# Turned tiles moved one place, LayerNorm sums of later tokens on ScalarE, last stores by SyncE and ScalarE

## The chip, the cores and the metric

The kernel runs on one core of one Trainium2 chip. The metric is the device time of one execution in microseconds (us). Engines are named as in the profile: PE (TensorE, matrix products), PEld (its weight loads), DVE (VectorE), ACT (ScalarE), POOL (GpSimd), SP (SyncE, which here only issues DMA transfers).

## The reference

Two rounds of attention and feed-forward over 2048 tokens of width 576. Each of the four steps adds to x what it computes from the normalised x. Attention has 32 heads of 18 columns; a token sees itself and seven earlier ones at distances 2, 4, ..., 14. The feed-forward part (FFN) has 4608 inner columns. All is fp32, with one core and batch 1.

```python
D, S, H, Dh, W, dil, F = 576, 2048, 32, 18, 8, 2, 4608

def _A_ref(x, wqkv, wo):
    qkv = (x @ wqkv).reshape(B, S, 3, H, Dh).transpose(2, 0, 3, 1, 4)
    q, k, v = qkv
    idx = arange(S)[:, None] - (arange(W) * dil)[None, :]          # masked where negative
    logits = einsum("bhsd,bhswd->bhsw", q, k[:, :, idx]) * Dh ** -0.5
    o = einsum("bhsw,bhswd->bhsd", softmax(logits), v[:, :, idx])
    return o.transpose(0, 2, 1, 3).reshape(B, S, D) @ wo

def _B_ref(x, w1, w2):
    return silu(x @ w1) @ w2

x = x + _A_ref(layernorm(x), wqkv, wo)
x = x + _B_ref(layernorm(x), w1, w2)
x = x + _A_ref(layernorm(x), wqkv, wo)      # the same weights again
x = x + _B_ref(layernorm(x), w1, w2)
```

## The kernel before

**Stages.** The tokens are cut into four chunks of 512, and a chunk into four tiles of 128 tokens. A stage s (0 to 7) is one chunk in one layer: s = 0 to 3 are the chunks of layer 0, 4 to 7 those of layer 1. A stage does LayerNorm, qkv (line 707), attention on DVE, the projection with its own transposes ("project", line 876), a second LayerNorm ("LN(s)" below), and the FFN. Every fp32 operand of a matmul is split into two f16 halves, and a product takes three f16 passes: high with high, high with low, low with high. A tile's normalised tokens yh (high and low half) are turned, that is transposed, before they can enter a product: by PE and a copy on ACT (lines 441 and 443) or by a DMA of SP (line 445).

**Chunk 0's stage carries more.** While attention of chunk 0 runs on DVE, PE computes qkv for chunks 1, 2 and 3 ahead (`qkv_ahead`, line 707 with `ra`, `rb`, `h` or `wo` as weights). So the LayerNorms of all four chunks (x, x1, x2, x3 in `front(0)`) come early, and DVE has the statistics of all of them. Then comes project(0), LN(0) and the first FFN.

**FFN.** Stages 0 to 2 use the plain form: line 1137 multiplies a tile of 128 inner columns (56 matmuls are four such tiles), ACT applies SiLU (line 1139), ACT and DVE split the result into halves (lines 1044 and 1046), and line 1150 accumulates the second product into `acc`, which DVE adds to x (line 883). From stage 3 on a cheaper form (`pair_z`, line 1064) uses prepared weights that `prepare` makes during the earlier stages. In the first FFN the weights are raw: POOL loads them (line 910), ACT squares and sums them for a scale (lines 931 and 933), PE adds over partitions (line 936), DVE rounds to powers of two (lines 413 to 415), then ACT and DVE write the two halves (lines 944 to 951).

**LayerNorm's forms.** `layer_norm(xs, prio, into, on_act, ...)`: with `on_act` False, DVE does the statistics (lines 469 and 470) and the normalisation (548, 553 and 428). With True, statistics are on DVE, and ACT shifts and scales (562 and 565), with the low half on DVE (428). With 2, ACT sums too: a Copy pass with an accumulator for the sum, the mean of all four tiles on DVE, and then a Square pass for the variance (the function `total`). `into` names the place that the turned tokens take.

**Places.** One large tile of SBUF (`rb`) is cut in several ways (`shared`); the cuts overlap, and a buffer may take a place only when whatever overlaps it has been read. XW is the size of one chunk's turned tokens. Chunks 0 to 3 of the qkv stage take the three places of "xa" in turn, (0, XW), (XW, 2XW), (2XW, 3XW), so that chunk 3 gets (XW, 2XW). The FFN's turned tokens take "x0", "x1", "x2". In LN the first write of a chunk (the key "hold" on the first operation of the normalisation) already claims the place.

**Order.** No order is written by hand. Every operation is given to a planner (`Plan`) with an engine, a cost in us, what it reads and writes, a priority and buffers. The planner simulates the engines, picks for each engine the ready operation of best priority, and gives the buffers out in turns. The order in which it picks is the order of each engine's queue. On the chip an engine runs its queue in that order and waits only for data and places.

Of the kernel before, what the change touches and what calls it, by code (L numbers as in the profile page):

```python
# [278 lines left out]
def sliding_attention_silu_ffn(ctx: ExitStack, tc: tile.TileContext, x, wqkv, wo, w1, w2, out):  # L279
# [637 lines left out]
    def raw_split(f0, prio):  # L917
# [11 lines left out]
        for f in fs:  # L929
            a, b = raws[f]  # L930
            op("ACT", 0.95, lambda f=f: nc.scalar.activation(junk[:, 0:640], fl(ra(f)), AF.Square,
                                                             accum_out=accw[:, f, 0:1]), [a], [("accw", f, 0)], prio)
            op("ACT", 0.9, lambda f=f: nc.scalar.activation(junk[:, 0:D], rb(f), AF.Square,
# [8 lines left out]
        for f, (wa, wb) in zip(fs, wab):  # L942
            a, b = raws[f]
            op("ACT", 0.82, lambda f=f, wa=wa: nc.scalar.activation(T(wa)[:, 0:5, :], ra(f), AF.Copy,
                                                                    scale=s12[:, f, 0:1]), [a, ("s12", f)], [(wa, 0)], prio)
            op("DVE", 0.9, lambda f=f, wa=wa: nc.vector.scalar_tensor_tensor(
                T(wa)[:, 5:10, :], ra(f), s12[:, f, 0:1], T(wa)[:, 0:5, :], op0=ALU.mult, op1=ALU.subtract),
               [a, (wa, 0), ("s12", f)], [(wa, 1)], prio)
            op("ACT", 0.77, lambda f=f, wb=wb: nc.scalar.activation(T(wb)[:, 0, :], rb(f), AF.Copy,
                                                                    scale=s12[:, f, 1:2]), [b, ("s12", f)], [(wb, 0)], prio)  # L950
            op("DVE", 0.83, lambda f=f, wb=wb: nc.vector.scalar_tensor_tensor(
# [147 lines left out]

    def ffn(s, xT, xs):  # L1100
# [4 lines left out]
        for g in range(NFT // n):  # L1105
# [8 lines left out]
            for f in range(g * n, (g + 1) * n):  # L1114
# [24 lines left out]
                op("ACT", 0.7, lambda z=z, hs=hs, f=f: nc.scalar.activation(T(hs), T(z), AF.Silu, scale=r12[:, f, 0:1]),  # L1139
                   [z, ("s12", f)], [(hs, 0), (hs, 1)], pd, table="silu")  # L1140
# [18 lines left out]
        for j in range(NJ):  # L1159
# [3 lines left out]
            else:  # L1163
                op("POOL", 0.6, lambda j=j: nc.gpsimd.dma_start(x_rows(out, c, j), T(xs[j])), [xs[j]], [], pd,  # L1164
                   nbytes=P * D * 4)
# [93 lines left out]
```

## Time and profile before

| | before |
|---|---|
| median of 3 runs | 2170.06 us (2168.5 to 2170.9) |
| profiled execution, device time | 2170.76 us |
| its span in the profile | 2169.0 us |
| mean granted clock of PE | 0.995 |
| PE busy | 2116.9 us (98%), 15676 matmuls |
| DVE busy | 1623.5 us (75%) |
| ACT busy | 958.4 us (44%) |
| POOL busy | 455.3 us (21%) |

The span runs from the first to the last instruction that the profile shows. Busy times are sums over one engine. A row of the waits names the engine that waited, line and operand, after `<-` who released it, and then the total, how often, and the longest. In a timeline the first number is the start, the second the duration of the whole group `xN` of equal instructions, and the bracket at the end the idle time before it with its releaser. A row of instruction groups ends with busy time and mean ns of one, and with the idle time of the engine before them. Rows that name a `DRAIN` or a semaphore belong to an engine's sequencer and not to its busy time.

### The profile page before, as it was taken

Reading aid. Unit: us, or ns where it says so; the run is one execution under the profiler, and the core shown is the slowest. Engines: PE = TensorE matmul, PEld = TensorE weight load, DVE = VectorE, ACT = ScalarE, POOL = GpSimd, SP = SyncE. Lnnn points to the kernel's source line nnn. Section 1 sums busy time; section 2 is a strip of 40 time slices with the busy share of each in tenths; the row PEclk is TensorE's granted clock in tenths of the full one; section 3 lists DMA queues with packets and bytes.
Section 4 is the critical chain, followed back from the end, with each engine's and each line's share of the span. In section 5 each row is a group of like instructions: output and inputs, shape, how many; then the busy total and the mean of one; then the engine's idle time right before and its main releaser. Section 6 shows DMA issues by size and latency. Waiting matters only on the chain.

```text
span 2169.0 us, 39537 instructions
## 1 busy us (share of the span) xinstructions
PE 2116.9 (98%) x15676; PEld 1529.5 (71%) x15676; DVE 1623.5 (75%) x2541; ACT 958.4 (44%) x1685; POOL 455.3 (21%) x713
## 2 busy tenths in 40 slices
PE   5999899999999999999999999999999999999998
PEld 3555556656666665677787778877788778888886
DVE  7999799999999986679974798629974398733332
ACT  7544877553244434364432544324434345324431
POOL 3234455310355654631000110000000100000000
PEclk9999899999999999999999999999999999999999
DMA  7778567776688879796458855676557665555541
GB/s 198 198 204 270 194 223 249 239 226 198 198 239 261 254 180 236 232 298 201 130 160 221 250 171 166 151 256 180 155 150 222 195 188 153 156 161 178 181 150 41
DMA packets 296217, 429.08 MB, mean 198 GB/s; under 512 B 150480, under 2 KB 182076, under 8 KB 291552
## 3 DMA queue, kind: packets, MB, share of 16 engines
q1 hardware_dynamic: 251360, 301.53, 48.2%
q0 software_dynamic: 42656, 123.93, 18.2%
q8 instruction: 122, 2.00, 0.4%
q10 hardware_dynamic: 2016, 1.11, 0.2%
q14 instruction: 63, 0.52, 0.1%
HBM read 303.19 MB, written 72.40 MB: 173 GB/s over the span
## 4 chain that ended last, share of the span: by engine, by line
PE 65%; issue 18%; DVE 8%; DMA 5%; ACT 1%; POOL 1%; SPq 0%; ACTq 0%; POOLq 0%; DVEq 0%
PE acc L1150 28%; PE z L1064 14%; PE z L1137 13%; PE z L707 7%; PE acc L876 3%; DMA rb<-in_B_w_dram 1%; DVE lg L808 1%; DVE pr L837 1%; DMA w<-in_B_w_dram 1%; DVE pr L844 1%; DMA w<-wts 1%; DVE pr L804 1%; DVE yh L428 1%; DMA w<-in_A_wqkv_dram 0%; DVE st L469 0%
## 5 line engine op out<-in xcount | busy, mean ns | idle before, releaser
L1150 PE MATMUL acc<-w,h 128*128 128x288 f16 x6912 | 881.5, 286 | 0.2 <-DVE x L883 0.2
L1150 PEld LDWEIGHTS <-h 128*128 128x128 f16 x6912 | 676.1, 98 | 172.5 <-issue 0.4
L1064 PE MATMUL z<-rb,w 128*128 128x256 f16 (+1 forms) x4410 | 518.9, 272 | 2.4 <-ACT hs L1069 1.4
L1064 PEld LDWEIGHTS <-w 128*128 128x128 f16 (+1 forms) x4410 | 429.0, 97 | 68.7 <-issue 1.9
L1137 PE MATMUL z<-rb,w 128*128 128x512 f16 x1512 | 334.5, 381 | 2.7 <-ACT rb L443 1.4
L883 DVE SCALAR_TENSOR_TENSOR x<-acc,d,x 128x576 f32<-128x576 f32 x192 | 156.2, 814 | 174.4 <-PE acc L1150 173.7
L1044 ACT ACTIVATE h<-hs,sh 128x512 f16<-128x512 f32 x288 | 201.2, 718 | 181.0 <-PE acc L1150 175.4
L707 PEld LDWEIGHTS <-rb 128*128 128x128 f16 x1792 | 175.6, 98 | 149.2 <-issue 6.6
L1137 PEld LDWEIGHTS <-w 128*128 128x128 f16 x1512 | 148.4, 98 | 176.5 <-issue 6.4
L1046 DVE SCALAR_TENSOR_TENSOR h<-hs,sh,h 128x512 f16<-128x512 f32 x288 | 208.6, 747 | 63.0 <-ACT h L1044 61.8
L1072 DVE TENSOR_TENSOR hs<-z,hs 128x256 f32<-128x256 f32 x270 | 110.2, 419 | 175.8 <-PE z L1064 105.6
L707 PE MATMUL z<-ra,rb 128*128 128x432 f16 x1176 | 224.8, 347 | 2.3 <-ACT qt L775 2.2
L1069 ACT ACTIVATE hs<-z 128x256 f32<-128x256 f32 x270 | 97.6, 379 | 228.8 <-PE z L1064 218.7
L837 DVE TENSOR_TENSOR pr<-kv,pe 128x1152 f32<-128x1152 f32 x128 | 170.2, 1351 | 0.7
L804 DVE TENSOR_TENSOR pr<-qt,kv 128x2304 f32<-128x2304 f32 x64 | 163.2, 2551 | 5.1 <-DMA kv<-kv 3.5
L808 DVE TENSOR_REDUCE lg<-pr 128x128 f32<-128x2304 f32 x64 | 162.9, 2545 | 0.5
L1076 ACT ACTIVATE hs<-hs,dt 128x256 f32<-128x256 f32 (+1 forms) x180 | 109.5, 612 | 89.7 <-DVE hs L1072 89.4
L1139 ACT ACTIVATE hs<-z,r 128x512 f32<-128x512 f32 x108 | 73.9, 685 | 167.1 <-PE z L1137 166.4
L1164 POOL DMA_DIRECT2D out_dram<-x x16 | 8.8, 552 | 652.0 <-DVE x L883 652.0
L844 DVE TENSOR_TENSOR pr<-pr 128x1152 f32<-128x1152 f32 (+1 forms) x128 | 135.1, 1055 | 3.2
L876 PE MATMUL acc<-wo,oT 128*128 128x288 f16 x896 | 113.5, 286 | 0.0
L773 ACT ACTIVATE kv<-z,ru 128x288 f32<-128x288 f32 x80 | 39.6, 495 | 156.1 <-PE z L707 156.1
(212 smaller groups left out, 1785.6 us busy)
## 6 DMA issues: line engine op xcount, KB each, us to landing
w<-wts SPq DMA_DIRECT2D x270, 320.0 KB
w<-w2s SPq DMA_DIRECT2D x252, 288.0 KB
w<-w1s SPq DMA_DIRECT2D x72, 320.0 KB
kv<-kd SPq DMA_DIRECT2D x12, 1584.0 KB
ra<-wqs SPq DMA_DIRECT2D x17, 1080.0 KB
w<-wts SPq DMA_DIRECT2D x90, 160.0 KB
w1s<-w POOLq DMA_DIRECT2D x36, 320.0 KB, 3.6
w2s<-w POOLq DMA_DIRECT2D x36, 288.0 KB, 4.1
```

Of the source, the lines that this page charges most:

```text
L707: nc.tensor.matmul(T(m)[:, :3 * UC], a, b, start=n == 0, stop=n == len(pl) - 1)
L804: nc.vector.tensor_tensor(T(pr), T(qt)[:, j:j + 2, None, :].to_broadcast([P, 2, W, UC]), win(T(kv), j, 2), op=ALU.mult)
L808: nc.vector.tensor_reduce(T(lg)[:, j:j + 2].rearrange("p a w h -> p (a w h)"), T(pr).rearrange("p a w (h d) -> p (a w h) d", d=DH), axis=A ...
L837: nc.vector.tensor_tensor(T(pr)[:, a].rearrange("p w (h d) -> p w h d", d=DH), v, T(pe)[:, j + a, :, :, None].to_broadcast([P, W, UH, DH]) ...
L844: nc.vector.tensor_tensor(t[:, :, 0:h, :], t[:, :, 0:h, :], t[:, :, h:2 * h, :], op=ALU.add)
L876: nc.tensor.matmul(T(acc)[:, h, 0:288], a, b[:, h * 288:(h + 1) * 288], start=n == 0, stop=n == len(pl) - 1)
L883: nc.vector.scalar_tensor_tensor(t, T(acc)[:, :, 0:288], d, t, op0=ALU.mult, op1=ALU.add)
L1044: op("ACT", 0.72, lambda: nc.scalar.activation(T(h)[:, 0, :], T(hs), AF.Copy, scale=sh[:, f:f + 1]), [(hs, 0), (hs, 1), key], [(h, 0)], pd)
L1046: op("DVE", 0.75, lambda: nc.vector.scalar_tensor_tensor(T(h)[:, 1, :], T(hs), sh[:, f:f + 1], T(h)[:, 0, :], op0=ALU.mult, op1=ALU.subtract),
L1064: nc.tensor.matmul(T(z)[:, 0:HT], T(w[m // 2])[0:q, 2 * j + m % 2 if m < 6 else j, :], T(xT)[0:q, 5 * c + i, :], start=first and n == 0, s ...
L1137: nc.tensor.matmul(T(z), v, u, start=m == 0, stop=m == len(pl) - 1)
L1150: nc.tensor.matmul(T(acc)[:, h, 0:288], T(hb[q])[:, a, j * P:(j + 1) * P], T(wbs[q][0])[:, w, h * 288:(h + 1) * 288], start=q == 0 and m = ...
```

## The change

There are four parts.

1. The places. Chunk 3's turned tokens get a tag of their own, "xb", with the place that they had before. Chunk 0's turned tokens for the FFN move from (XW, 2XW) to (0, XW), which was chunk 0's place in the qkv stage, and x1 and x2 change accordingly, with the third place of the prepared weights "pw".
2. LayerNorm. The sums of chunk 2 (ahead), chunk 3 and LN(0) go from DVE to ACT (`on_act` 2); LN(0)'s normalisation goes to ACT too, but for the low half.
3. The planner's costs are written anew for some twenty operations (a few lines are shown). They change no operation, but the whole order.
4. The end. The last tile's accumulation is done by column halves, each with its own add and its own store, one by SP and one by ACT; the other three stores of the last chunk go from POOL to SP.

```diff
-        ("x0", [(XW, 2 * XW)], cut(9), True),
-        ("x1", [(0, XW)], cut(9), True),
-        ("x2", [(35 * HT, 35 * HT + XW)], cut(9), True),
+        ("xb", [(XW, 2 * XW)], cut(9), True),
+        ("x0", [(0, XW)], cut(9), True),
+        ("x1", [(XW, 2 * XW)], cut(9), True),
+        ("x2", [(2 * XW, 3 * XW)], cut(9), True),
...
-        ("pw", [("ra", 0, 30 * P), (3 * XW, 3 * XW + 30 * P), (XW, XW + 30 * P)], lambda v: v, True)])
+        ("pw", [("ra", 0, 30 * P), (3 * XW, 3 * XW + 30 * P), (0, 30 * P)], lambda v: v, True)])
...
-                op("DVE", 1.15, lambda j=j: stats(j), [xs[j]], [(st, j), (mv, j)], prio)
+                op("DVE", 0.95, lambda j=j: stats(j), [xs[j]], [(st, j), (mv, j)], prio)
...
-            op("DVE", 1.25 if blk == 0 else 0.9, soft_a, [], lgs + [mx], pr_)
+            op("DVE", 1.43 if blk == 0 else 1.02, soft_a, [], lgs + [mx], pr_)
...
+    def last(acc, j, g, n, hb, wbs, pp, pd, xs):
+        for h in range(2):
+            sl = slice(h * 288, (h + 1) * 288)
+            def mm(h=h, sl=sl):
+                for q in range(n):
+                    for m, (a, w) in enumerate(((0, 0), (0, 1), (1, 0))):
+                        nc.tensor.matmul(T(acc)[:, h, 0:288], T(hb[q])[:, a, j * P:(j + 1) * P], T(wbs[q][0])[:, w, sl],
+                                         start=q == 0 and m == 0, stop=q == n - 1 and m == 2)
+            op("PE", 0.37 * n, mm, ..., [(acc, h)], pp)
+            op("DVE", 0.46, lambda h=h, sl=sl: nc.vector.scalar_tensor_tensor(
+                T(xs[j])[:, sl], T(acc)[:, h, 0:288], d2[:, g:g + 1], T(xs[j])[:, sl], op0=ALU.mult, op1=ALU.add),
+               [(acc, h), ("sh", g), xs[j]], [(xs[j], h)], pd)
...
+            op(("SP", "ACT")[h], 0.5, lambda h=h, sl=sl, o=o: (nc.sync, nc.scalar)[h].dma_start(o, T(xs[j])[:, sl]),
+               [(xs[j], h)], [], pd, nbytes=P * D * 2)
...
+                if s == NL * NC - 1 and g == NFT // n - 1 and j == NJ - 1:
+                    last(acc, j, g, n, hb, wbs, pp + LATE, pd, xs)
+                    continue
...
-            else:
+            elif s < NL * NC - 1:
                 op("POOL", 0.6, lambda j=j: nc.gpsimd.dma_start(x_rows(out, c, j), T(xs[j])), [xs[j]], [], pd,
                    nbytes=P * D * 4)
+            elif j < NJ - 1:
+                op("SP", 0.5, lambda j=j: nc.sync.dma_start(x_rows(out, c, j), T(xs[j])), [xs[j]], [], pd,
+                   nbytes=P * D * 4)
...
-            x2 = layer_norm(load_x(2, -2.0, gate[3:4]), -2.0, "xa", True, PE_LN[2])
+            x2 = layer_norm(load_x(2, -2.0, gate[3:4]), -2.0, "xa", 2, PE_LN[2])
...
-            x3 = layer_norm(load_x(3, -1.2, gate[11:12]), -1.2, "xa", True, PE_LN[3])
+            x3 = layer_norm(load_x(3, -1.2, gate[11:12]), -1.2, "xb", 2, PE_LN[3])
...
-        XT[s] = layer_norm(X[s], s - 1.0, "xt" if s >= SF else f"x{s}", (False, True, False, False)[min(s, 3)], s == 0)
+        XT[s] = layer_norm(X[s], s - 1.0, "xt" if s >= SF else f"x{s}", (2, True, False, False)[min(s, 3)], s == 0)
```

**How the order moves at LN(0).** ACT's queue before, from the last copies of chunk 3's qkv (`hs<-z`, line 720) on; `rb<-acc` copies a turned tile, `junk,accw<-` squares raw weights:

```order
L720 ACTIVATE hs_119<-z_129,ru 128x432
L720 ACTIVATE hs_122<-z_130,ru 128x432
L443 ACTIVATE rb<-acc_134 128x9x128
L931 ACTIVATE junk,accw<-rb 128x640
L443 ACTIVATE rb<-acc_133 128x9x128
L933 ACTIVATE junk,accw<-rb 128x576
```

The four copies of turned tiles stand behind all qkv copies. The same place in the changed kernel, ACT (lines are one or two numbers higher; `y<-x,nt` and `yh<-y,nt` are the normalisation):

```order
L721 ACTIVATE hs_119<-z_130,ru 128x432
L444 ACTIVATE rb<-acc_134 128x9x128
L563 ACTIVATE y_87<-x_69,nt_127 128x576
L566 ACTIVATE yh_89<-y_87,nt_127 128x576
L721 ACTIVATE hs_121<-z_129,ru 128x432
L444 ACTIVATE rb<-acc_133 128x9x128
L721 ACTIVATE hs_120<-z_130,ru 128x432
L444 ACTIVATE rb<-acc_134 128x9x128
L828 ACTIVATE pe_84<-lg_82 128x256
L1160 ACT_TABLE_LOAD
L1160 ACTIVATE hs_119<-z_129,r_296 128x512
```

Copies of qkv tiles and of turned tiles now alternate, and the first SiLU (line 1160) follows the last of them behind one exponential of attention(1). DVE before, from the end of LN(0)'s Newton steps (`nt`) to the first tile's low half (line 428):

```order
L496 SCALAR_TENSOR_TENSOR nt_127<-nt_127 128x4
L837 TENSOR_TENSOR pr_79<-kv_76,pe_83 128x1152 x2
L844 TENSOR_TENSOR pr_79<-pr_79 128x2x576
L844 TENSOR_TENSOR pr_79<-pr_79 128x2x288
L845 TENSOR_TENSOR o_78<-pr_79 128x2x144
L837 TENSOR_TENSOR pr_79<-kv_76,pe_83 128x1152 x2
L548 TENSOR_SCALAR y_87<-x_66,mv_125,nt_127 128x576
L553 TENSOR_SCALAR yh_88<-y_87 128x576
L428 SCALAR_TENSOR_TENSOR yh_88<-y_87,yh_88 128x512
```

DVE in the changed kernel, the same place:

```order
L497 SCALAR_TENSOR_TENSOR nt_127<-nt_127 128x4
L845 TENSOR_TENSOR pr_79<-pr_79 128x2x576
L845 TENSOR_TENSOR pr_79<-pr_79 128x2x288
L846 TENSOR_TENSOR o_78<-pr_79 128x2x144
L429 SCALAR_TENSOR_TENSOR yh_88<-y_87,nt_127,yh_88 128x512
L429 SCALAR_TENSOR_TENSOR yh_88<-y_87,nt_127,yh_88 128x64
L805 TENSOR_TENSOR pr_79<-qt_81,kv_77 128x2304
L429 SCALAR_TENSOR_TENSOR yh_89<-y_87,nt_127,yh_89 128x512
```

Less attention work stands between Newton's last step and the first tile, and the two high-half operations are gone from DVE.

**Behind the first FFN tiles.** ACT in the changed kernel, from the third SiLU on; `w_94` and `w_100` are the weights of the fifth and sixth FFN tile:

```order
L1160 ACTIVATE hs_121<-z_129,r_296 128x512
L934 ACTIVATE junk,accw<-rb 128x576
L932 ACTIVATE junk,accw<-ra 128x640
L1160 ACTIVATE hs_120<-z_130,r_296 128x512
L934 ACTIVATE junk,accw<-rb 128x576
L945 ACTIVATE w_94<-rb,s_295 128x640
L950 ACTIVATE w_104<-rb,s_295 128x576
L945 ACTIVATE w_100<-rb,s_295 128x640
```

The weights of the fifth tile are written behind the fourth SiLU and the last square; before, they were written ahead of the first SiLU. PE's two sums for these scales (line 937) stand behind the fourth tile's matmuls.

**The end.** SP's last rows in the changed kernel (before, its queue ended with the two weight loads, and POOL's with four stores of 128x576):

```order
L894 DMA w_106<-w2s_227 128x1152
L894 DMA w_109<-w2s_228 128x1152
L1191 DMA out_dram<-x_70 128x576
L1191 DMA out_dram<-x_71 128x576
L1191 DMA out_dram<-x_72 128x576
L1118 DMA out_dram<-x_73 128x288
```

The other half of x_73 is ACT's last row.

More of the change, by code (lines that the diff above doesn't have):

```diff
@@ L809, in red @@
                                             T(pr).rearrange("p a w (h d) -> p (a w h) d", d=DH), axis=AX.X, op=ALU.add)
-                op("DVE", 2.57, mul, keys + [(qt, j), (qt, j + 1)], [pr], pr_)
-                op("DVE", 2.57, red, [pr], [(lg, j)], pr_)
+                op("DVE", 2.5, mul, keys + [(qt, j), (qt, j + 1)], [pr], pr_)
+                op("DVE", 2.5, red, [pr], [(lg, j)], pr_)
             def soft_a(lg=lg, mx=mx):
@@ L930, in raw_split @@
             a, b = raws[f]
-            op("ACT", 0.95, lambda f=f: nc.scalar.activation(junk[:, 0:640], fl(ra(f)), AF.Square,
+            op("ACT", 0.88, lambda f=f: nc.scalar.activation(junk[:, 0:640], fl(ra(f)), AF.Square,
                                                              accum_out=accw[:, f, 0:1]), [a], [("accw", f, 0)], prio)
-            op("ACT", 0.9, lambda f=f: nc.scalar.activation(junk[:, 0:D], rb(f), AF.Square,
+            op("ACT", 0.82, lambda f=f: nc.scalar.activation(junk[:, 0:D], rb(f), AF.Square,
                                                             accum_out=accw[:, f, 1:2]), [b], [("accw", f, 1)], prio)
@@ L943, in raw_split @@
             a, b = raws[f]
[L944 removed]
+            op("ACT", 0.74, lambda f=f, wa=wa: nc.scalar.activation(T(wa)[:, 0:5, :], ra(f), AF.Copy,
                                                                     scale=s12[:, f, 0:1]), [a, ("s12", f)], [(wa, 0)], prio)
[L946 removed]
+            op("DVE", 0.81, lambda f=f, wa=wa: nc.vector.scalar_tensor_tensor(
                 T(wa)[:, 5:10, :], ra(f), s12[:, f, 0:1], T(wa)[:, 0:5, :], op0=ALU.mult, op1=ALU.subtract),
                [a, (wa, 0), ("s12", f)], [(wa, 1)], prio)
[L949 removed]
+            op("ACT", 0.69, lambda f=f, wb=wb: nc.scalar.activation(T(wb)[:, 0, :], rb(f), AF.Copy,
                                                                     scale=s12[:, f, 1:2]), [b, ("s12", f)], [(wb, 0)], prio)
[L951 removed]
+            op("DVE", 0.74, lambda f=f, wb=wb: nc.vector.scalar_tensor_tensor(
                 T(wb)[:, 1, :], rb(f), s12[:, f, 1:2], T(wb)[:, 0, :], op0=ALU.mult, op1=ALU.subtract),
@@ L1043, in halves @@
     def halves(f, hs, h, key, pd):
-        op("ACT", 0.72, lambda: nc.scalar.activation(T(h)[:, 0, :], T(hs), AF.Copy, scale=sh[:, f:f + 1]),
+        op("ACT", 0.66, lambda: nc.scalar.activation(T(h)[:, 0, :], T(hs), AF.Copy, scale=sh[:, f:f + 1]),
            [(hs, 0), (hs, 1), key], [(h, 0)], pd)
-        op("DVE", 0.75, lambda: nc.vector.scalar_tensor_tensor(
+        op("DVE", 0.69, lambda: nc.vector.scalar_tensor_tensor(
             T(h)[:, 1, :], T(hs), sh[:, f:f + 1], T(h)[:, 0, :], op0=ALU.mult, op1=ALU.subtract),
@@ L1071, in add @@
         def add(z, t, s, k):
-            op("DVE", 0.43, lambda: nc.vector.tensor_tensor(T(t)[:, s], T(z)[:, 0:HT], T(t)[:, s], op=ALU.add),
+            op("DVE", 0.36, lambda: nc.vector.tensor_tensor(T(t)[:, s], T(z)[:, 0:HT], T(t)[:, s], op=ALU.add),
                [z], [(t, k)], pd - 0.2)
@@ L1098, in pair_z @@
             halves(f, t, h, key, pd)
+    def last(acc, j, g, n, hb, wbs, pp, pd, xs):
[6 more added lines that the diff above has]
+                                         start=q == 0 and m == 0, stop=q == n - 1 and m == 2)
+            op("PE", 0.37 * n, mm, [(hb[q], a) for q in range(n) for a in range(2)] + [k for q in range(n) for k in wbs[q][1]],
+               [(acc, h)], pp)
+            op("DVE", 0.46, lambda h=h, sl=sl: nc.vector.scalar_tensor_tensor(
+                T(xs[j])[:, sl], T(acc)[:, h, 0:288], d2[:, g:g + 1], T(xs[j])[:, sl], op0=ALU.mult, op1=ALU.add),
+               [(acc, h), ("sh", g), xs[j]], [(xs[j], h)], pd)
+            o = x_rows(out, NC - 1, j)
+            o = bass.AP(tensor=o.tensor, offset=o.offset + h * 288, ap=[o.ap[0], [1, 288]])
+            op(("SP", "ACT")[h], 0.5, lambda h=h, sl=sl, o=o: (nc.sync, nc.scalar)[h].dma_start(o, T(xs[j])[:, sl]),
+               [(xs[j], h)], [], pd, nbytes=P * D * 2)
     def ffn(s, xT, xs):
```

4 lines of the change are left out of this document (2 added, 2 removed).

## The prediction

> **What bounds the kernel now.** I read the busy time of each engine by stretches first, because it shows in one table where TensorE does not work. Columns: stretch and its length; busy time and instructions of PE, weight loads, DVE, ACT and POOL; granted clock; DMA share; GB/s.
>
> ```profile
> 0.00:200.00 200.00, 175.65 (x1026) 99.23 (x1027) 180.58 (x316) 112.64 (x220) 61.53 (x100) 1.00 0.76 216
> 150.00:200.00 50.00, 48.89 (x332) 30.71 (x331) 48.94 (x67) 25.90 (x45) 18.52 (x33) 1.00 0.75 254
> 200.00:250.00 50.00, 37.27 (x188) 18.54 (x187) 40.22 (x69) 27.50 (x47) 20.17 (x34) 0.83 0.56 182
> 250.00:2150.00 1900.00, 1895.22 (x14396) 1405.01 (x14395) 1400.33 (x2156) 818.25 (x1419) 371.98 (x578) 1.00 0.67 198
> 2150.00:2169.00 19.00, 8.73 (x72) 6.75 (x69) 2.40 (x3) 0.00 (x0) 1.62 (x3) 0.87 0.11 47
> ```
>
> For 1900 us in the middle PE is the bound: it misses 4.8 us in all. No matmul is removed, so only the 52 us in which PE idles can be won: 24.4 before 200, 12.7 from 200 to 250, 10.3 at the end. The waits of PE and its timeline say what the 12.7 are (columns of the waits: total, times, longest).
>
> ```profile
> PE acc L441 <- DVE yh L553: 8.1, 4, 3.1
> PE z L1137 <- ACT rb L443: 1.4, 1, 1.4
> ```
> ```profile
> 202.35 10.38 PE L707 MATMUL z<-ra,rb 128*128 128x432 f16 x56
> 214.55 0.40 PE L441 MATMUL acc<-ident,yh 128*128 128x128 f16 x4 [1.82 <-DVE yh L553]
> 215.41 0.45 PE L441 MATMUL acc<-ident,yh 128*128 128x128 f16 x5 [0.47 <-DVE yh L428]
> 227.79 0.61 PE L441 MATMUL acc<-ident,yh 128*128 128x128 f16 x4 [0.34 <-DVE yh L553]
> 230.87 14.44 PE L1137 MATMUL z<-rb,w 128*128 128x512 f16 x56 [1.43 <-ACT rb L443]
> 245.15 0.28 PE L936 MATMUL z<-accw,ones 128*128 128x4 f32 x2
> 245.29 6.20 PE L1137 MATMUL z<-rb,w 128*128 128x512 f16 x28
> ```
>
> After the last of chunk 3's qkv tiles (212.7) PE has only chunk 0's LN transposes, and DVE hands them over one at a time until the first FFN matmul at 230.87. That matmul stretch is slow too: its 56 matmuls take 14.44, where the next 28 take 6.20, so 12.4 for 56. The 2.0 are the low clock (0.83 in this stretch). Why DVE is late stands in its own timeline:
>
> ```profile
> 205.47 0.16 DVE L496 SCALAR_TENSOR_TENSOR nt<-nt 128x4 f32<-128x4 f32 x1
> 205.55 2.62 DVE L837 TENSOR_TENSOR pr<-kv,pe 128x1152 f32<-128x1152 f32 x2
> 213.43 0.57 DVE L548 TENSOR_SCALAR y<-x,mv,nt 128x576 f32<-128x576 f32 x1
> 227.84 0.83 DVE L428 SCALAR_TENSOR_TENSOR yh<-y,yh 128x512 f16<-128x512 f32 x2
> ```
>
> The statistics are complete at 205.6, yet the normalisation starts at 213.43, behind attention work and 0.7 after the last matmul that reads chunk 3's turned tokens, whose place chunk 0's were to take. That is the "hold" in the code.
>
> **The change part by part.** *The new places and ACT for LN(0).* The order now has LN(0)'s transposes between the last four qkv tiles, and the first FFN matmul right behind the fourth transposition. Up to PE's 1536th row both orders read nearly alike, and there project(0) begins earlier by four qkv tiles:
>
> ```profile
> 164.51 10.38 PE L707 MATMUL z<-rb 128*128 128x432 f16 x56
> 174.73 1.17 PE L441 MATMUL acc<-ident,yh 128*128 128x128 f16 x18
> 173.33 1.80 DVE L428 SCALAR_TENSOR_TENSOR yh<-o,so,yh 128x512 f16<-128x512 f32 x4
> ```
>
> So PE asks for project(0)'s first tile at 164.5 and not at 174.7. Can DVE deliver? Durations (busy total, mean ns; the row of POOL is a load with its time to landing):
>
> ```profile
> L469 DVE BATCH_NORM_STATS2 st<-x 128x6 f32<-128x288 f32 x128 | 52.1, 449 | 7.0 <-DMA x<-in_A_x_dram 5.5
> L470 DVE BATCH_NORM_AGGREGATE mv<-st 128x2 f32<-128x12 f32 x64 | 13.4, 209 | 2.2
> L804 DVE TENSOR_TENSOR pr<-qt,kv 128x2304 f32<-128x2304 f32 x64 | 163.2, 2551 | 5.1 <-DMA kv<-kv 3.5 <-DMA w<-wts 1.0
> L808 DVE TENSOR_REDUCE lg<-pr 128x128 f32<-128x2304 f32 x64 | 162.9, 2545 | 0.5
> L933 ACT ACTIVATE junk<-rb 128x576 f16<-128x576 f32 x32 | 21.6, 676 | 5.9 <-DMA rb<-in_B_w_dram 5.6
> L933 ACT ACTIVATION_READ_ACCUMULATOR junk<-rb 128x1 f32 x32 | 6.0, 187 | 0.0
> L443 ACT ACTIVATE rb<-acc 128x1152 f16<-128x1152 f16 x8 | 8.9, 1118 | 7.1 <-PE acc L441 7.1
> ra<-in_B_w_dram POOLq DMA_DIRECT2D x15, 256.0 KB, 5.0
> L1139 ACT ACTIVATE hs<-z,r 128x512 f32<-128x512 f32 x108 | 73.9, 685 | 167.1 <-PE z L1137 166.4
> L944 ACT ACTIVATE w<-rb,s 128x640 f16<-128x640 f32 x17 | 13.5, 817 | 16.5 <-DVE s L414 16.5
> L946 DVE SCALAR_TENSOR_TENSOR w<-rb,s,w 128x640 f16<-128x640 f32 x17 | 14.6, 877 | 0.0
> ```
>
> Eight tiles' statistics leave DVE ahead of that place, 8 x (2 x 0.449 + 0.209) = 8.9, and one pair of attention(1) now stands behind it, 2.55 + 2.55 = 5.1. Together 14.0, if DVE is the bound there, which it is (48.94 of 50 busy). DVE begins at 159.3, before PE asks. From there to LN(0)'s last low halves DVE worked 55.3 (173.33 to 228.67). It loses four tiles' statistics (4.4) and the first half of the normalisation (one L548 of 0.57 and one half of that size for each tile, some 4.3) and gains one L804, so about 49, which ends at 208.8, or near 213 if each step waits for PE's projection first. ACT gets 24 passes over 576 columns; none is in the trace, and the nearest row is the square over 576 columns, 0.68 + 0.19 = 0.87, so 21 us, and about 6 for LN(0)'s eight normalising passes. ACT is busy for 112.64 of the first 200, and I price them at nothing; if they queue, the lower end is what follows.
>
> PE then has no gap up to the FFN: 164.51 plus its old work to 212.73 (48.2, of which 1.1 was idle), plus four transpositions at the full clock (0.40 + 0.45 each as in the first tile, 3.4), plus one copy of 1.12 on ACT: 216.1 (without the idle) to 217.2. I take 216.2, which is 14.7 earlier. The first 56 matmuls at full clock save 2.0 more.
>
> Something new is late next. Behind the fourth FFN tile stand two L936 (two weight scales), and the fifth tile's weights hang on ACT, which must first do the fourth SiLU. From the end of the fourth tile: SiLU 0.69, last square 0.87, L936 0.28, the power of two on DVE about 0.4 (three operations of some 0.16), ACT's first half 0.82, DVE's rest 0.88, together 3.9. In the trace of before the fifth tile does not wait (245.29 follows 245.15), so the bounds are 0 and 3.9; the order makes all six steps follow each other, so I take 3.9. One of the squares reads a raw weight that POOL loads into a place of chunk 3's last qkv tile: free at about 213, landed 5.0 later, 218, which is before the fourth tile ends at 228; the load costs nothing. A gap of that length may also bring the low clock back, 0 to 2.0; I take 1.0. The gain at the start is 14.7 + 2.0 - 3.9 - 1.0 = 11.8, between 9 and 16.7.
>
> *The planner's new costs* move everything behind that. Summed over the orders at this trace's durations, PE reaches project(1) after 49 us and project(2) after 36 us less matmul work than before, while DVE's work ahead of them falls by 43 and 19. PE waits for little there now (4.8 in 1900), so new waits can only cost. The bounds are 0 and the rival's 25 below; I take 2, nearer zero, since the new costs only write each operation at about the duration it has in this trace.
>
> *The end.*
>
> ```profile
> 2139.83 18.91 PE L1150 MATMUL acc<-w,h 128*128 128x288 f16 x153
> 2158.77 0.82 DVE L883 SCALAR_TENSOR_TENSOR x<-acc,d,x 128x576 f32<-128x576 f32 x1 [3.59 <-PE acc L1150]
> 2159.89 0.54 POOL L1164 DMA_DIRECT2D out_dram<-x  x1 [3.87 <-DVE x L883]
> L1255 POOLq DRAIN  x3: 46/98/8229, 2159.9 to 2168.6; - x3
> L845 DVE TENSOR_TENSOR o<-pr 128x288 f32<-128x288 f32 x64 | 29.3, 458 | 2.6
> DMA to landing us min/median/max: 2.3/2.4/5.4
> ```
>
> (The last row: the stores of line 1164.) The last matmul ends at 2158.7. The store is issued at 2159.89 and lands some 2.4 later, but POOL's DRAIN behind it takes 8.23 and ends at 2168.1; the span ends 0.9 later. With SP and ACT storing, POOL's last software store is chunk 6's, some 200 us earlier, and its drain is hidden. The new end: half a vector operation 0.46 after 2158.74, issue 0.3 later (as 2159.59 to 2159.89), landing 2.4 to 5.4, then 0.9: 2162.8 to 2165.8. The gain is 3.2 to 6.2; I take 5.6, by the median landing and some slack. SP and ACT have nothing queued behind these stores. The 18 + 18 matmuls are the same 36 as before and cost nothing more.
>
> A rule speaks against this. The Trainium skill, "DMA: Bandwidth & Descriptors", sections "Specifications" and "Issuing engines are not separate DMA queues", gives a first byte after about 1 us by GpSimd and 0.6 by SP or ACT, and says that issuing from several engines only saves the time of issue. The Trainium skill, "VectorE: DVE Perf Modes", section "The DRAIN you can't avoid", calls the DRAINs around a kernel a constant 12 ns. By these the estimate of the tail's gain is 0.4, and with the half operation 0.8. The 8229 ns row differs from the second; no row here shows a store from SP or ACT at the end.
>
> Sum: -11.8 - 5.6 + 2 = -15.4 from the profiled execution's 2170.76 (span 2169.0 and 1.76 around it), 2155.4; the median of the runs is 0.7 lower than that execution, 2170.06, so 2154.7. I forecast **2154.5**.
>
> **The rivals.** *B: the start gives little back.* Weight scales late and a low clock at the first FFN tiles, as at 230.87, and a few such gaps in the planner's new order: 3.9 + 2.0 twice over and 2 of others leave a start gain of 6: 2160. For it: ACT carries 27 us more. Against: ACT is under 60% busy.
>
> *C: slower, DVE late at project(2).*
>
> ```profile
> 566.86 5.31 PE L876 MATMUL acc<-wo,oT 128*128 128x288 f16 x42
> 554.45 0.95 DVE L428 SCALAR_TENSOR_TENSOR yh<-o,so,yh 128x512 f16<-128x512 f32 x2
> ```
>
> PE would ask for it 36 + 13 earlier, at 518; DVE, if it has only 19 less to do, delivers at 535 and the DMA turn follows (12.4 after that row now, some 8 needed): 543, a wait of 25, so 2154.5 + 25 = 2179.5. It decides from a wait of 16 to 20 on. Against: between 200 and 250 DVE itself idles for 9.8, which go with the gap at LN(0).
>
> *D: the tail stays,* since the final drain does not hang on the software store: 2154.5 + 4.8 = 2159.3. This is about what the rules of the Trainium skill named above would give.
>
> *E: the change doesn't do it:* LN(0) stays late, because DVE's attention work and not the place delays it (from 205.6 to 213.4 DVE was busy); only the tail comes, 2165.
>
> *F: better:* the fifth tile does not wait, nothing new waits: -16.7 - 6.2 = 2147.2.
>
> **How the numbers follow.** Forecast 0.52 (its own range 2151 to 2158), B 0.16, D 0.08, F 0.08, E 0.08, C 0.08. The bound of what can be told from no change is 0.2%, 4.3 us: 2165.7 and 2174.4. The range reaches from F's 2148 to 2166, which leaves out C and the outer parts of E and F, under 0.2. Faster: all but C and half of E, with some of B's tail, 0.85; same 0.08; slower 0.07.
>
> **What would show it.** In the trace after, PE's transposes of LN(0) lie between qkv tiles without a wait over 0.5, the first FFN matmul starts at 215 to 218, a gap of about 4 stands ahead of the fifth tile, the sixth tile ends near 239 (245.29 + 6.20 now), and the stretch from the last matmul to the end is 4 to 7 (10.3 now) with POOL's long DRAIN far ahead of it. Waits of PE over 10 us at project(1) or (2), or a tail above 9, would make me wrong.

## The result and the profile after

The changed kernel is slower: 2182.07 us median (2179.9 to 2188.0, 4 runs) against 2170.36 (2168.5 to 2170.9, 4 runs), a ratio of 1.0053 with a 95% interval of 1.0038 to 1.0069. The forecast was 2154.5. A profile shows one execution: in e2, e3 and e14 below it is the longest of the run and in e1, e7 and e13 the shortest, and the ratio of e4 leaves out one execution of 5787.15.

The same stretches as before, in the changed kernel's profiled execution (2180.06 us, span 2177.9; columns as above):

```profile
0.00:200.00 200.00, 165.86 (x965) 93.56 (x966) 168.62 (x281) 124.87 (x254) 58.73 (x95) 0.99 0.75 207
200.00:250.00 50.00, 45.68 (x249) 23.51 (x248) 47.05 (x68) 36.65 (x64) 18.90 (x33) 0.93 0.56 186
250.00:2150.00 1900.00, 1883.34 (x14271) 1393.32 (x14270) 1380.99 (x2140) 818.95 (x1419) 375.61 (x583) 1.00 0.68 198
2150.00:2178.00 28.00, 24.10 (x197) 19.01 (x195) 7.88 (x11) 2.79 (x4) 0.00 (x0) 0.97 0.18 64
```

PE's idle time, stretch by stretch: before 200 us it rose from 24.4 to 34.1; from 200 to 250 it fell from 12.7 to 4.3, as forecast; from 250 to 2150 it rose from 4.8 to 16.7; at the end it fell from 10.3 to 3.9. Together 6.9 more, and PE's own work takes 2.1 more (2119.0 against 2116.9 for the same 15676 matmuls). That is the 8.9 by which the spans differ. PE's waits name the new places (some rows are left out):

```profile
PE z L708 <- ACT w L721: 8.8, 3, 4.3
...
PE z L1065 <- DMA w<-wts: 4.9, 4, 2.6
PE z L1158 <- ACT hs L1160: 4.2, 3, 2.4
PE z L1065 <- ACT hs L1070: 3.2, 6, 0.8
PE z L937 <- ACT junk L934: 2.2, 2, 1.3
...
PE acc L442 <- DVE yh L429: 1.4, 4, 0.5
```

The four waits of 8.1 us for `yh` at LN(0) are gone, and no other has come there: the 1.4 of the last row, and 6.6 of a row left out, fall in the first 100 us, in chunk 0's first LayerNorm, where before had nearly the same. The largest new wait is for ACT's copies of qkv tiles. (Also left out is the wait ahead of the first matmul of all, 13.5 here and 12.3 before.) PE's timeline shows both, the waits first and then LN(0):

```profile
123.95 2.71 PE L708 MATMUL z<-rb 128*128 128x432 f16 x14 [0.63 <-ACT w L721]
130.54 7.83 PE L708 MATMUL z<-rb 128*128 128x432 f16 x42 [3.87 <-ACT w L721]
152.90 11.81 PE L708 MATMUL z<-h,rb 128*128 128x432 f16 x56 [4.31 <-ACT w L721]
...
174.90 1.17 PE L442 MATMUL acc<-ident,yh 128*128 128x128 f16 x18
...
224.94 0.67 PE L442 MATMUL acc<-ident,yh 128*128 128x128 f16 x9
226.84 12.25 PE L1158 MATMUL z<-rb,w 128*128 128x512 f16 x56 [1.23 <-ACT rb L444]
238.92 0.28 PE L937 MATMUL z<-accw,ones 128*128 128x4 f32 x2
240.52 0.39 PE L937 MATMUL z<-accw,ones 128*128 128x4 f32 x2 [1.32 <-ACT junk L934]
241.38 0.61 PE L1158 MATMUL z<-rb,w 128*128 128x512 f16 x1 [0.47 <-ACT w L945]
243.29 8.30 PE L1158 MATMUL z<-rb,w 128*128 128x512 f16 x27 [1.31 <-DVE w L947]
```

Project(0)'s transposes have moved ahead of four qkv tiles, and yet they start at 174.90, at the same time as before (174.73): the 10.2 us of work that now stand behind them were lost in waits ahead of them. From there PE runs to the first FFN matmul with hardly a gap and at full clock (56 matmuls in 12.25, before 14.44). Then come the gap at the fifth tile and slow matmuls behind it (27 in 8.30, at full clock 6.0). The sixth tile ends at 251.6, before at 251.5: at this point nothing at all is gained. Behind it, up to the last matmul, the changed kernel takes 15.3 more (1922.5 against 1907.2) for the same 14458 matmuls: 11.9 more idle time, and 3.4 more of PE's own work.

What ACT did while PE waited at 124 to 153 stands in ACT's timeline:

```profile
123.30 0.60 ACT L721 ACTIVATE w<-z,ru 128x432 f32<-128x432 f32 x1
129.21 0.77 ACT L566 ACTIVATE yh<-y,nt 128x576 f16<-128x576 f32 x1 [5.30 <-DMA rb<-yh]
129.89 0.60 ACT L721 ACTIVATE w<-z,ru 128x432 f32<-128x432 f32 x1
...
151.56 0.68 ACT L934 ACTIVATE junk<-w 128x576 f16<-128x576 f32 x1 [7.43 <-DMA w<-in_B_w_dram]
```

ACT was not busy. Twice an operation at the head of its queue waited for a transfer, 5.30 for a `yh` buffer that SP's transposition still read and 7.43 for a raw weight, and the copy of a finished qkv tile stood behind it. PE has two z buffers and stops when neither is copied out.

The end came as forecast:

```profile
2169.53 4.57 PE L1109 MATMUL acc<-w,h 128*128 128x288 f16 x36
2174.14 0.94 DVE L1113 SCALAR_TENSOR_TENSOR x<-acc,d,x 128x288 f32<-128x288 f32 x2 [3.59 <-PE acc L1109]
2174.68 0.33 SPq L1118 DMA_DIRECT2D out_dram<-x  x1
2175.11 0.36 ACTq L1118 DMA_DIRECT2D out_dram<-x  x1
L1282 POOLq DRAIN  x3: 46/106/8392, 1971.9 to 2177.7; - x3
```

From the last matmul (2174.1) to the end of the span are 3.8 us, before 10.3. POOL's longest DRAIN still takes 8.39, but it begins at 1971.9, behind stage 6's stores.

### The profile page after: what moved, and what is told of

It is laid out like the page before. It is cut to its first block, busy times and chain, and to the rows that moved or that the text cites. A ratio compares the mean times of both kernels' runs of the same rounds, so it can differ in the third digit from the quotient of the medians.

```text
span 2177.9 us, 39553 instructions
## 1 busy us (share of the span) xinstructions
PE 2119.0 (97%) x15676; PEld 1529.4 (70%) x15676; DVE 1604.5 (74%) x2499; ACT 983.3 (45%) x1739; POOL 453.2 (21%) x709
## 4 chain that ended last, share of the span: by engine, by line
PE 73%; DVE 11%; DMA 9%; issue 2%; ACT 2%; POOL 2%; SPq 0%; ACTq 0%; DVEq 0%; POOLq 0%
PE acc L1174 33%; PE z L1065 20%; PE z L1158 9%; PE z L708 7%; PE acc L877 3%; DMA w<-wts 1%; DVE pr L805 1%; DMA rb<-yh 1%; DVE lg L809 1%; DVE pr L838 1%; DMA rb<-in_B_w_dram 1%; DVE pr L845 1%; DVE rb L1020 1%; DMA w<-in_B_w_dram 1%; DVE x L884 1%
## 5 line engine op out<-in xcount | busy, mean ns | idle before, releaser
L805 DVE TENSOR_TENSOR pr<-qt,kv 128x2304 f32<-128x2304 f32 x64 | 163.3, 2551 | 5.9 <-DMA kv<-kv 5.4
L786 POOL DMA_DIRECT2D kv<-kv x80 | 42.5, 537 | 326.2 <-ACT qt L776 325.1
L877 PEld LDWEIGHTS <-oT 128*128 128x128 f16 x896 | 87.4, 98 | 26.0 <-ACT oT L444 2.5
```

What stands on the lines that cost most here:

```text
L805: nc.vector.tensor_tensor(T(pr), T(qt)[:, j:j + 2, None, :].to_broadcast([P, 2, W, UC]), win(T(kv), j, 2), op=ALU.mult)
L877: nc.tensor.matmul(T(acc)[:, h, 0:288], a, b[:, h * 288:(h + 1) * 288], start=n == 0, stop=n == len(pl) - 1)
```

## The experiments

Three theories were tried. *ACT's queue*: the sums and the new order on ACT put operations that wait for transfers ahead of copies that PE needs. *The costs*: the planner's new costs give an order with many small waits. *Absorption*: DVE and ACT limit PE between 250 and 900 anyway, so that an earlier first FFN is taken back. Behind each run stands its ratio to the kernel before on the same chip; "behind 250" is PE's idle time from 250 to 2150 in its profile, 1900 less the busy time (4.8 before, 16.7 after). The ratio is not exactly the quotient of the two medians. In the diffs, words and `...` stand for code that is left out.

**Parts of the change one by one.** First the end alone:

```diff
 (before)
+    last(...) for the last tile; stores of the last chunk by SP, its last half by ACT
```

> Only the end is changed (last tile by halves, last stores by SP and ACT); old places, old LayerNorm forms, old costs. The order of every engine stays that of before up to its last rows. Both theories: the stretch from the last matmul to the end falls from 10.3 to about 3.8 us as in the changed kernel, nothing else moves, 2164 us. If the gain at the end hung on something else in the changed kernel, 2170.

2166.29, ratio 0.9974 (0.9962 to 0.9986). Behind 250: 4.7. The end of its profile, from 2150 on (14 us, the last 0.7 of them past the span's end):

```profile
2150.00:2164.00 14.00, 9.40 (x77) 7.27 (x75) 2.58 (x4) 0.00 (x0) 0.00 (x0) 0.93 0.17 64
```

PE idles for 3.9 within the span, as in the changed kernel. The end is worth 5.7 to 6.7 us by itself, and needs nothing of the rest.

```diff
 (before)
+    all new costs of the planner; places, LayerNorm forms and end as before
```

> Only the planner's new costs; places, LayerNorm forms and end as before. Theory 1 (the new costs make the order worse): PE's idle time behind 250 us grows from 4.8 to some 15, and ACT's queue blocks PE between 100 and 165 as in the changed kernel (some 9 us), 2180 to 2192. Theory 2 (the sums on ACT make the blocks, the costs are harmless): PE waits for nothing new, 2168 to 2173.

2192.67, ratio 1.0082 (1.0065 to 1.0099), behind 250: 21.8. The costs alone lose more than the whole change does. No single wait carries it:

```profile
PE z L1064 <- DMA w<-wts: 5.6, 3, 3.3
PE acc L1150 <- DVE x L883: 4.1, 4, 1.9
PE z L936 <- ACT junk L933: 4.1, 2, 3.9
PE z L1064 <- ACT hs L1069: 4.1, 7, 0.8
PE z L707 <- ACT qt L775: 3.8, 2, 3.0
```

Between 100 and 165 its PE waits only 3.0, so the two blocks of the changed kernel are not made by the costs alone.

```diff
 (after)
-    all new costs of the planner (old ones put back)
```

> The whole change but for the new costs: places, sums on ACT, end. Theory 1 (costs): no blocks at 120 to 155, first FFN matmul at 216 to 220, little idle behind 250, 2153 to 2160. Theory 2 (sums on ACT): PE still waits some 9 us for ACT's copies of qkv tiles between 100 and 165, first FFN matmul near 227, and with the shorter end 2163 to 2170.

2166.78, ratio 0.9969 (0.9958 to 0.9980): the time that theory 2 gave, but not for its reason. PE waits only 3.0 for ACT's copies at 124 and 149, the first FFN matmul starts at 220.1, but behind 250 PE idles 16.1. So with the old costs too the new plan loses behind what it won ahead, and what is left of the gain is about that of the end alone. *The costs* as I had put it is therefore not the whole story. Nor is *ACT's queue*: e3 has all the sums on ACT and waits 3.0 for those copies, the changed kernel 8.8. The two kernels differ in the costs alone. Of the 8.2 between their profiled spans (2169.7 and 2177.9), 7.2 is idle time of PE before 200 us (27.0 and 34.1), and behind 250 it idles nearly the same (16.1 and 16.7). So the long blocks take the sums and the new costs together, while the loss behind 250 comes with the old costs too.

```diff
 (before)
+        ("xb", ...), ("x0", [(0, XW)], ...), ("x1", [(XW, 2 * XW)], ...), ("x2", [(2 * XW, 3 * XW)], ...), "pw" as in the change
+            x3 = layer_norm(..., "xb", True, ...)
```

> Only the places (x0 in chunk 0's old place, xb for chunk 3, x1, x2 and pw moved); LayerNorm forms, costs and end as before. Two of LN(0)'s four transpositions then stand ahead of the last qkv tiles. If the hold on the place is what made PE wait at LN(0), the first FFN matmul comes 3 to 8 us before 230.87 and the time is 2163 to 2168. If DVE's attention work delays the tiles anyway, 2169 to 2171.

2170.95, ratio 0.9989 (0.9974 to 1.0003). In the profiled run the hold was indeed most of what delayed LN(0): the first FFN matmul starts at 221.6, 9.3 earlier. DVE still delays the last tile: PE waits 3.41 for its high half, which the change gives to ACT. But behind 250 PE idles 12.6 instead of 4.8, and the time is the same as before within its interval.

**ACT's queue.**

```diff
 (after, L = the planner's order)
+    later = {362: (350, 353, 357, 358), 409: (395,)}   # scaling of chunk 3's third tile behind two copies of qkv tiles,
+                                                        # square of a raw weight behind three
```

> The changed kernel with three operations of ACT moved back in its queue (and the two of DVE and SP between them): the scaling of chunk 3's third tile, which waited 5.3 us for a transposition by DMA, stands behind two more copies of qkv tiles, and the square of a raw weight, which waited 7.4 us for its load, behind three. If it is the line in ACT's queue that held PE at 124 to 153: PE's waits for those copies fall from 8.8 to under 2, the first FFN matmul comes at 218 to 221 (226.8 now), and the time falls by what is not absorbed behind, 2172 to 2179. If PE was held by something else: no change, 2180 to 2184.

2177.97, ratio 1.0027 (1.0016 to 1.0038). The wait for `w` is no longer among PE's waits over 1 us, and the timeline moves as expected:

```profile
163.26 0.38 PE L442 MATMUL acc<-ident,yh 128*128 128x128 f16 x4
...
217.31 4.91 PE L1158 MATMUL z<-rb,w 128*128 128x512 f16 x22 [1.23 <-ACT rb L444]
```

Project(0) starts at 163.3 and the first FFN matmul at 217.3; the forecast had 164.5 and 216.2. So the two operations at the head of ACT's queue account for all that was missing at the start. The profiled span is 7.4 shorter than the changed kernel's (2170.5 against 2177.9), and the ratio falls from 1.0053 to 1.0027 (the medians are 4.1 apart). Behind 250 it idles 18.2: this part of the loss has another cause.

**Is an early start absorbed, or is it the plan?** To tell these apart, the order of before is kept and only LN(0) is moved, by hand, behind the planner.

```diff
 (before with the new end, L = the planner's order, x0, x1, x2 and pw placed as in the change after planning)
+    early = {ln0[4]: (5, 6, 9, 10), done[45]: (7, 8, 13, 14), done[46]: (11, 12, 17, 18), done[47]: (15, 16, 19, 20)}
+    # LN(0)'s norm, halves, turn and copy of each tile behind Newton's last step and the last qkv tiles
```

> The order of before with the new end; only LN(0)'s four tiles are moved by hand, behind Newton's last step on DVE and between the last four qkv tiles on PE, with chunk 0's turned tokens in chunk 0's old place. No LayerNorm form and no cost changes. Compared with the new end alone: first FFN matmul near 216 to 218 instead of 231. Theory 1 (the order behind decides; a gain at LN(0) carries to the end if the order behind it stays): 9 to 14 us below the new end alone, 2152 to 2157. Theory 2 (DVE and ACT are the bound between 250 and 900, so an earlier start is absorbed there whatever the order): new waits of PE behind 250 of 7 to 14 us, 2163 to 2167.

2165.36, ratio 0.9970 (0.9958 to 0.9981), no better than the new end alone. This move missed its aim and so decided nothing: it put ACT's copy of a turned tile ahead of the copy of a qkv tile (PE waits 1.73 twice), and left the scale of the fifth tile's weights ahead of the first FFN matmul:

```profile
227.22 0.59 PE L936 MATMUL z<-accw,ones 128*128 128x4 f32 x2 [5.95 <-ACT junk L933]
```

The first FFN matmul starts at 227.7. The second try reorders 95 operations (POOL's loads of raw weights, the squares, LN(0), the copies, the first four SiLUs):

```diff
 (as the last one, but)
+    L = L[:546] + [L[i] for i in hand] + L[641:]    # hand: the numbers 546 to 640 in an order written out
```

> Order of before with the new end; 95 operations around LN(0) are reordered by hand (LN(0)'s tiles between the last four qkv tiles, copies of qkv tiles ahead of those of turned tiles on ACT, the two weight scales behind the first FFN tile), all else stays. First FFN matmul at 216 to 219. If an earlier FFN start carries to the end when the order behind it stays as it was: 9 to 14 us below the new end alone, 2152 to 2158, and PE's idle time behind the first FFN matmul stays at 5 to 9. If DVE or ACT absorb it: that idle time grows to 14 to 20, 2162 to 2167.

2157.95, ratio 0.9937 (0.9920 to 0.9953), where the new end alone has 0.9974: about 8 us more.

```profile
209.51 0.68 PE L441 MATMUL acc<-ident,yh 128*128 128x128 f16 x9
210.03 2.72 PE L707 MATMUL z<-ra,rb 128*128 128x432 f16 x14
...
218.56 3.18 PE L1157 MATMUL z<-rb,w 128*128 128x512 f16 x14 [1.75 <-ACT rb L443]
221.58 0.28 PE L936 MATMUL z<-accw,ones 128*128 128x4 f32 x2
221.72 12.25 PE L1157 MATMUL z<-rb,w 128*128 128x512 f16 x56
...
236.96 4.57 PE L1173 MATMUL acc<-w,h 128*128 128x288 f16 x36
245.84 0.59 PE L936 MATMUL z<-accw,ones 128*128 128x4 f32 x2 [4.30 <-ACT junk L933]
...
256.48 0.39 PE L936 MATMUL z<-accw,ones 128*128 128x4 f32 x2 [1.22 <-ACT junk L933]
...
250.00:2150.00 1900.00, 1894.16 (x14388) 1404.69 (x14386) 1397.18 (x2149) 811.01 (x1405) 368.31 (x569) 1.00 0.67 198
```

The first FFN matmul starts at 218.6, without a gap at the fifth tile, and the second product starts at 236.96, 14.4 before 251.33. Of that 5.5 go at once in two waits for the next weights' squares (4.30 and 1.22), and 2.2 in slower matmuls behind the first of them (54 in 8.98, at 256.73 in 6.78); behind 250 PE idles 5.8 in all, 1.0 more than before. The 6.7 that are left agree with the profiled span, 6.9 shorter than that of the new end alone (2156.4 against 2163.3). So what is left of an early start at 263 carries to the end when the order behind it stays. *Absorption* is refuted for a start of this size; what e4, with no other cost and no other LayerNorm form, lost behind 250 was lost by its new plan, and the same is the likely reading of e3. Of the 17.4 that the prediction expected of LN(0) and the end (11.8 and 5.6) some 13.7 are here (0.0063 of 2172), without the sums on ACT and without new costs.

**What makes a new plan worse?** Two of the costs were changed by a hundredth or two, with nothing else:

```diff
 (before)
-        op("ACT", 0.72, lambda: nc.scalar.activation(T(h)[:, 0, :], ...
+        op("ACT", 0.73, lambda: nc.scalar.activation(T(h)[:, 0, :], ...
```

> Before, with one number changed by a hundredth: the planner's cost of the first half of h on ACT, 0.72 to 0.73. The order stays word for word as before until PE's 3960th row (about 330 us) and differs behind. If the values of the new costs do the harm: 2168 to 2174. If any new plan of the planner is worse than the one that before has: PE's idle time behind the first FFN matmul grows from 5 to 10 to 20, 2176 to 2190.

2172.36, ratio 1.0004 (0.9995 to 1.0014), behind 250: 5.8.

```diff
 (before)
-            op("DVE", 1.1, soft_b, [], [pe, sm], pr_)
+            op("DVE", 1.12, soft_b, [], [pe, sm], pr_)
```

> The same with another number: the cost of the second part of the softmax on DVE, 1.10 to 1.12; the order stays as before until PE's 4391st row. If the values matter: 2168 to 2174. If any new plan is worse: 2176 to 2190.

2176.73, ratio 1.0026 (1.0016 to 1.0037), behind 250: 7.8. These two new plans cost 0 and 0.26%, not the 0.8% of the new costs. They are only two, and they share the order of before for a long way; e4, with the old costs, idled 7.8 more behind 250 than before. Then the new costs in groups, first the raised ones and then the lowered ones:

```diff
 (before)
+            soft_a 1.25 to 1.43 (0.9 to 1.02), soft_b 1.1 to 1.38
```

> Before with two of the new costs alone, those that are raised (softmax on DVE 1.25 to 1.43 and 1.1 to 1.38). If the lowered costs do the harm (the planner believes that results are there earlier than they are): 2168 to 2175. If the raised ones do: 2180 to 2193.

2176.80, ratio 1.0016 (1.0005 to 1.0028), behind 250: 9.3.

```diff
 (before)
+            all other new costs: statistics, products, squares, halves, add, SiLU, all lowered
```

> Before with all the other new costs, nearly all lowered (halves, squares, adds, SiLU, statistics). If the lowered costs do the harm: 2180 to 2193, with new waits of PE for DVE and ACT results of under 1 us each and for weights. If the raised ones do: 2168 to 2175.

2191.52, ratio 1.0086 (1.0069 to 1.0103), behind 250: 16.3. Of the two groups the lowered one carries the loss, as far as one plan of each can tell. It was split once more:

```diff
 (before)
+        halves on ACT 0.72 to 0.66 and on DVE 0.75 to 0.69, add 0.43 to 0.36, SiLU 0.7 to 0.64
```

> Before with the four new costs of the FFN alone (halves on ACT 0.72 to 0.66 and on DVE 0.75 to 0.69, add 0.43 to 0.36, SiLU 0.70 to 0.64); the order stays as before until PE's 2869th row. If these carry the loss of the lowered costs: PE's idle time behind the first FFN matmul grows from 5 to about 15, 2180 to 2192. If the losses are of new plans as such: like the two nudges, 2171 to 2178.

2212.77, ratio 1.0177 (1.0157 to 1.0197), behind 250: 39.3, the worst of all. Three of its waits:

```profile
475.72 20.33 PE L1137 MATMUL z<-rb,w 128*128 128x512 f16 x84 [9.27 <-DMA rb<-yh]
575.14 5.28 PE L876 MATMUL acc<-wo,oT 128*128 128x288 f16 x28 [4.12 <-DMA oT<-yh]
1005.63 5.61 PE L1064 MATMUL z<-rb,w 128*128 128x256 f16 x35 [2.58 <-DMA w<-wts]
```

They are waits for transfers (turned tiles by SP, prepared weights). Idle time is not all of the loss: PE's busy time for the same 15676 matmuls is 2130.1 here and 2125.9 in e2, at granted clocks of 0.988 and 0.991, against 2116.9 at 0.995 before.

```diff
 (before)
+        squares and halves of the raw weights, six costs, each lower by 0.07 to 0.09
```

> Before with the six new costs of the raw weights' squares and halves alone (each lower by 0.07 to 0.09); the order stays as before until PE's 2728th row. If these carry the loss: 2180 to 2192. If not: 2171 to 2178.

2188.65, ratio 1.0072 (1.0054 to 1.0089), behind 250: 17.2. Each group of lowered costs loses by itself, and the two together (e10) lose less than the first alone: the losses do not add. Last, the time that the planner allows from one engine to the next:

```diff
 (before with all new costs)
-    LAT = 0.2
+    LAT = 0.3
```

> Before with all new costs, and the planner's time from the end of an operation to its use raised from 0.2 to 0.3 us. If the new costs do harm because they leave no room for the time from one engine to the next: much of the 20 us comes back, 2172 to 2182. If it is not that: 2185 to 2197 as with the new costs alone.

2191.89, ratio 1.0086 (1.0068 to 1.0103), like the new costs alone; behind 250: 14.8. This longer time between engines does not mend it.

**Were the new costs nearer to the measured durations?** The trace of before says no for every lowered one. These rows (mean ns behind the busy time) belong to the FFN's halves and add and to the second part of the softmax:

```profile
L1044 ACT ACTIVATE h<-hs,sh 128x512 f16<-128x512 f32 x288 | 201.2, 718 | 181.0 <-PE acc L1150 175.4
L1046 DVE SCALAR_TENSOR_TENSOR h<-hs,sh,h 128x512 f16<-128x512 f32 x288 | 208.6, 747 | 63.0 <-ACT h L1044 61.8
L1072 DVE TENSOR_TENSOR hs<-z,hs 128x256 f32<-128x256 f32 x270 | 110.2, 419 | 175.8 <-PE z L1064 105.6 <-ACT hs L1069 69.3 <-ACT qt L775 0.4
...
L822 DVE TENSOR_REDUCE mx<-pe 128x32 f32<-128x256 f32 x32 | 19.6, 612 | 15.0 <-ACT pe L827 14.9
L823 DVE RECIPROCAL mx<-mx 128x32 f32<-128x32 f32 x32 | 11.3, 353 | 1.1
L824 DVE TENSOR_TENSOR pe<-pe,mx 128x256 f32<-128x256 f32 x32 | 13.6, 425 | 1.1
```

| operation | measured in before | old cost | new cost |
|---|---|---|---|
| first half of h on ACT (L1044) | 0.718 | 0.72 | 0.66 |
| second half of h on DVE (L1046) | 0.747 | 0.75 | 0.69 |
| add (L1072) | 0.419 | 0.43 | 0.36 |
| SiLU (L1139) | 0.685 | 0.70 | 0.64 |
| statistics of a tile (2 x L469 and L470) | 1.107 | 1.15 | 0.95 |
| second part of the softmax (L822 to L824) | 1.390 | 1.10 | 1.38 |

The old value is within 5% of the measured one wherever the new one is lower, and the new one lies 2 to 14% below it (the rows that the table leaves out included); only the raised softmax costs came nearer. The lowered costs are close to another time, the one after which an engine starts its next independent operation: two L946 at 304.97 take 1.67 together, so the second begins some 0.79 after the first, where the new cost is 0.81 and one takes 0.88. But the planner takes an operation's cost also as the time until its result is there. That results planned too early make the orders worse fits the raised and the lowered group, but it is not shown: e13 adds 0.1 between engines, more than the 0.06 to 0.09 that most costs were lowered by, and gets nothing back.

What stays open is why these orders are worse. All five runs with lowered costs lost 0.7 to 1.8%, the raised set and the two nudges 0 to 0.3%. The longest waits of e14 are for transfers, whose times were planned as before. That does not hold for all: the longest wait of e15 behind 250 is 6.1 for an add of DVE (L1072), and that of e13 is 3.6 for the same line.

## Why the prediction was wrong, point by point

**LN(0) and the hold: right in mechanism and size.** The transposes lie between qkv tiles, PE waits for none of them there, and the clock stays full for the first 56 matmuls (12.25). With the two blocks taken out the first FFN matmul starts at 217.3 (forecast 216.2).

**"I price them at nothing": the step that failed at the start.** I asked whether ACT has time for 27 us more (it has: it is busy for 24.9 more in the whole run, and for 124.87 of the first 200), and not what would stand at the head of its queue. ACT's order had been read at LN(0) and behind, not between 100 and 160, where the scaling of chunk 3's third tile and a raw weight's square wait for transfers ahead of the copies that free PE's z buffers. The term was put at 0. PE waits 8.8 for these copies, and the 56 matmuls behind the longest of the waits take 11.81 in place of 10.38: together the 10.2 by which project(0) should have come earlier. A part of the 8.8 belongs to the new costs, since with the old ones (e3) the same sums cost a wait of 3.0. The start was to gain 11.8, and at the sixth tile's end it has gained nothing. A row for a warning was there: in before the square of a raw weight waits 2.84 for its transfer (ACT, 139.93), at the head of the queue from which PE's two z buffers are copied out.

**The fifth tile: right.** Forecast a gap of 3.9 and 1.0 for the low clock, 4.9 together; measured 1.32 + 0.47 + 1.31 = 3.1 of waits and 2.3 of low clock (8.30 for 27 matmuls, 6.0 at full clock), 5.4 together. The two errors partly cancel, which is luck.

**"I take 2, nearer zero, since the new costs only write each operation at about the duration it has": the step that failed most.** Its bounds were 0 and 25. From the sixth tile to the last matmul the changed kernel loses 15.3, of which 11.9 is idle time. The reason given was false by rows that stood in the prediction: SiLU takes 0.685 and went from 0.70 to 0.64, a tile's statistics take 1.107 and went from 1.15 to 0.95. The costs alone lose 0.82% (e2: 17.0 more idle time behind 250). And the term had the wrong owner as well: the order behind 250 moves with every part that the planner sees, not only with the costs, and e3, with the old ones, idles 16.1 there. Rival C had the sign, and named a single long wait at project(2); there is none: the waits are many and short, 2.6 at the longest, for weights, SiLU, halves and adds, and the projections behind 250 wait 1.0 in all.

**Two sums of the prediction do not come out as written.** Rival B's terms (twice 5.9, and 2) leave 2.9 of 16.7 and not 6, and DVE's 49 from 159.3 on end at 208.3 and not 208.8. Neither changes the forecast.

**The end: right, slightly better.** Forecast 5.6, measured 6.5 in the profile, 5.7 to 6.7 alone. The Trainium skill, "VectorE: DVE Perf Modes", section "The DRAIN you can't avoid", gives about 12 ns for the DRAINs of a kernel's preamble and postamble. POOL's DRAIN behind its last store takes 8229 to 8392 ns here; the trace decides. The gain is far above the 0.8 that the half operation and an earlier first byte were to give, so the end hung on this DRAIN.

**The chances.** 0.85 for faster came from adding the terms of a plan that had been read at two places. A part that rewrites the whole order should have had a wide term on the slow side.

## What to carry to other kernels

Where a table of costs drives a list scheduler (a planner that picks the best ready operation at each step), any change that it sees is a change of the whole order, and its price lies anywhere between nothing and 1.8% here. Hold each new cost against the measured duration before it goes in, and measure the table apart from the edit that it comes with. When work is moved to an engine that has time to spare, look at the head of its queue: one operation that waits for a transfer holds everything behind it, and PE stops as soon as its two output buffers are full. If a plan is good but for one place, move that place by hand and leave the rest: that gave 0.9937 with the second of two orders written by hand.

## What the runs showed of the hardware

POOL's DRAIN behind its last store takes 8.2 to 8.4 us, whether it stands at the end (2159.9 to 2168.1, before) or 200 us ahead of it (from 1971.9, after). Moving the last stores to SP and ACT hides it; with the last add split in two this is worth 0.26% alone.

A gap in PE's work can cost more than its length, but not always. The matmuls behind it took this much longer than the same number at full clock (in brackets):

| gap | matmuls behind it | longer by |
|---|---|---|
| 3.55 (e6_early_end) | 28 in 8.83 (6.20) | 2.6 |
| 3.1 in three pieces (changed kernel) | 27 in 8.30 (6.00) | 2.3 |
| 4.30 (e8_hand_end) | 54 in 8.98 (6.78) | 2.2 |
| 3.1 in three pieces (e7_unblock) | 27 in 7.44 (6.00) | 1.4 |
| 4.31 (changed kernel, at 152.90) | 56 in 11.81 (10.38) | 1.4 |
| 3.87 (changed kernel, at 130.54) | 42 in 7.83 (7.8) | 0 |
| 1.7 in two pieces (e3_oldcosts) | 27 in 6.00 (6.00) | 0 |
